# Attention and a two-layer network on one core: the first batch's q and k loaded in 2 KB runs and laid side by side by GpSimd

## The chip, the cores and the metric

The kernel runs on one core of one Trainium2 chip. The metric is the device time of one execution in microseconds, as the median of several runs. All arithmetic is 32-bit; matrix products run on TensorE (PE in the profile), the rest on VectorE (DVE), ScalarE (ACT) and GpSimd (POOL); SyncE (SP) issues nearly all loads and stores.

## What is computed

For 8 batches with 8 heads, 576 positions and 64 dimensions, two attentions are added: one over q, k and v averaged in groups of 4 (144 positions, its output repeated 4 times), and one over the 7 nearest positions. The result, 4608 rows of 512, goes through a layer of 2048 with a slope per column for negative values, and back to 512.

```python
q_d = q.reshape(B, H, Sd, 4, D).mean(axis=3)          # k_d, v_d alike
out_up = np.repeat(sm_attn(q_d, k_d, v_d), 4, axis=2)
mask = np.abs(pos[:, None] - pos[None, :]) < 4
scores = np.where(mask, scale * q @ k.T, -1e9)
out_local = softmax(scores) @ v
x = (out_up + out_local).transpose(0, 2, 1, 3).reshape(B * S, H * D)
h = x @ w_in
g = np.maximum(h, 0.0) + alpha * np.minimum(h, 0.0)
return g @ w_out
```

## The kernel before

**The steady part.** The 4608 rows go through the network in 18 chunks of 256 rows, each in 8 steps of 256 hidden columns: `hidden` (24 matmuls into h), `slopes` on ACT, `larger`, `split` into a high and a low part (gh, gl), `product` (24 matmuls into o). The weights are kept as high and low parts (wih, wil, woh, wol). They come as 64-bit numbers: `load_raw` brings a raw block (raw, 1 MB), and `make` turns it into the two parts: the absolute value on ACT (temp), two steps on DVE in `reach` (L198, L199), two in `bits` (L203, L204), the rounding on ACT (wih or woh, L209 or L213), the rest on DVE (wil or wol). Beside the matmuls run the attention of the later batches: `down` loads two heads' q, k and v (ld), adds them in fours on POOL (L74; s2q, s2k, s2v), and does the coarse attention; `local` does the near attention in units of 192 positions, mostly on DVE (qk, ls, lb, pv, x, xf).

**The first batch** is done ahead of all that by `first_batch`, as matrix products in four pairs of heads. For a pair hp, `load_pair` loads q and k of both heads into one tile fqk, so that the two heads' 64 dimensions lie side by side for each position, and v into fv; `load_windows` loads v once more in windows of 70 positions (vw). Then `pair`: fqk is transposed on PE (f0T for q, f1T for k); ACT copies it out into qb and kT; the near scores fs are 18 matmuls over a mask already in the bank; the coarse sums of q and k are adds on DVE (L466, L468), those of v L484 and L486; softmax (fmx, fp, fsm on DVE, exp on ACT), transposes (fpt, pT), the products with v (fdv, fpv), and the high and low parts xh and xl of the network's input.

**What sets the order.** The start, up to step 14, is not in a fixed order: a scheduler arranges each engine's queue by its own estimates, within what buffers and data allow. The loads are written in the order of `ORDER` ('i0 a0 a1 b0 o0 a2 b1 a3 b2 i1 b3 o1 i2': i and o are raw blocks of the input and output weight, a is `load_pair`, b is `load_windows`). Every engine works through its queue strictly in order, and SP holds a load until its buffer is free. From step 14 on the written order holds.

Of the kernel before, what the change touches and what calls it, by code (L numbers as in the profile page):

```python
# [9 lines left out]
F32 = mybir.dt.float32  # L10
# [13 lines left out]
HEAD = S * D  # L24
# [4 lines left out]
NWIN, WIN, KEYS = 9, 64, 70  # L29
# [23 lines left out]
def tile_attention_moe(ctx: ExitStack, tc: tile.TileContext, q, k, v, w_in, w_out, alpha, out):  # L53
    nc = tc.nc
# [3 lines left out]
    two = ctx.enter_context(tc.tile_pool(name="two", bufs=2))  # L58
# [80 lines left out]
    raws, turns = {}, [0, 0]  # L139
    weights_temp = []  # L140

    def load_raw(which, fp, blocks=(0, 1)):
        raw = raws.setdefault((which, fp), {})
        if fp < NP - 2:
            raw[None] = one.tile([128, 1024, 2], I32, tag=f"slot{turns[0] % 3}", name=f"raw{which}_{fp}")
            raw[0], raw[1] = raw[None][:, 0:512], raw[None][:, 512:1024]
            turns[0] += 1
        src = (w_in, w_out)[which].bitcast(I32)
        for c in blocks:
            if fp < NP - 2:  # L150
                dst = raw[None][:, 512 * c:512 * c + 512]
            elif fp == NP - 2:
                dst = raw[c] = late.tile([128, 512, 2], I32, tag="prod", name=f"raw{which}_{fp}{c}", bufs=PB)
            else:
                dst = raw[c] = late.tile([128, 512, 2], I32, tag=f"x{'hl'[c]}", name=f"raw{which}_{fp}{c}")
            if which == 0:
                nc.sync.dma_start(dst.rearrange("p (k a) b -> p k (a b)", k=2),
                                  bass.AP(src.tensor, 256 * c * 2 * DF + 512 * fp, [[2 * DF, 128], [256 * DF, 2], [1, 512]]))
            else:
                row = 256 * fp + 128 * c  # L160
                nc.sync.dma_start(dst.rearrange("p a b -> p (a b)"), src[row:row + 128, :])

    def weight_tiles(which, n):
        if n == 0 or (wi, wo)[which][0][n] is not None:
# [211 lines left out]
    def first_batch(st):  # L376
# [23 lines left out]
        qk, vt, vw = {}, {}, {}  # L400

        def load_pair(hp):
            qk[hp] = one.tile([72, 2, 8, 2, 64], F32, tag=f"spare{(4, 5, 0, 1)[hp]}", name=f"fqk{hp}")
            for i, src in enumerate((q, k)):
                for e in range(2):
                    nc.sync.dma_start(qk[hp][:, i, :, e, :],  # L406
                                      bass.AP(src.tensor, (2 * hp + e) * HEAD, [[512, 72], [64, 8], [1, 64]]))
            vt[hp] = st.tile([72, 2, 8, 64], F32, tag="vt", name=f"fv{hp}", bufs=3)
            nc.sync.dma_start(vt[hp].rearrange("p h t d -> p h (t d)"),
                              bass.AP(v.tensor, 2 * hp * HEAD, [[512, 72], [HEAD, 2], [1, 512]]))  # L410

        def load_windows(hp):
            vw[hp] = one.tile([KEYS, NWIN, 2, 64], F32, tag=f"spare{(6, 7, 2, 3)[hp]}", name=f"vw{hp}")
            for h2 in range(2):
                h = 2 * hp + h2
                if h == 0:
                    nc.vector.memset(vw[hp][0:3, 0, 0, :], 0.0)
                    nc.sync.dma_start(vw[hp][3:KEYS, 0, 0, :], bass.AP(v.tensor, 0, [[64, KEYS - 3], [1, 64]]))
                    nc.sync.dma_start(vw[hp][:, 1:, 0, :], bass.AP(v.tensor, (WIN - 3) * 64,
                                                                   [[64, KEYS], [WIN * 64, NWIN - 1], [1, 64]]))  # L420
                else:
                    nc.sync.dma_start(vw[hp][:, :, h2, :], bass.AP(v.tensor, h * HEAD - 3 * 64,
                                                                   [[64, KEYS], [WIN * 64, NWIN], [1, 64]]))

        def pair_bank(kind, name):
# [6 lines left out]
        def pair(hp):  # L432
# [100 lines left out]
            yield  # L533

        return load_pair, load_windows, pair


# [328 lines left out]
    with tc.tile_pool(name="start", bufs=1) as start:  # L866
        load_pair, load_windows, pair = first_batch(start)
        todo = [(w, fp) for fp in range(NP) for w in range(2)]
        for step in ORDER.split():
            kind, i = step[0], int(step[1])  # L870
            if kind in "io":
                load_raw("io".index(kind), i)
            else:
                (load_pair if kind == "a" else load_windows)(i)
        weights_temp.append(one.tile([128, 2, 1024], I32, tag="slot3", name="temp"))
        for hp in range(4):
            for _ in pair(hp):
                pass
        for fp in range(NP - 2):
            for which in range(2):  # L880
                if fp < N_EARLY:
                    if (which, fp) not in raws:
                        load_raw(which, fp)
                    for f in make(which, fp):
                        f()
        events = []

        def at(t, f, *args):
            events.append((t, len(events), f, args))

        down(1, 0, FIRST[0], 0.0, early=True)
# [12 lines left out]

    blocks = [(w, fp, c) for w in range(2) for fp in range(N_EARLY, NP) for c in range(2)]
    at(-1.98, load_raw, 0, N_EARLY)
    for fp in (NP - 2, NP - 1):
        at(-1.97, load_raw, 0, fp)
    at(-1.96, load_raw, 1, N_EARLY)
    t = T0_DEC  # L910
# [7 lines left out]
    for p in range(4 * (B - 1)):  # L918
        b, hp = 1 + p // 4, p % 4
# [17 lines left out]
    for u in range(3, 3 * B + 1):  # L937
# [7 lines left out]
        elif put:  # L945
            flip_at(u - 1, 0, begin[u] + 0.3, flip)
            put(0, when["before 0"])
            t = when["before 0"] + 0.25 if u == 4 else when["before 1"]
# [63 lines left out]
```

## Time and profile before

| | |
|---|---|
| median of 3 runs | 988.4 us (986.08 to 989.0) |
| profiled execution | 990.46 us, its span 988.6 us |
| PE busy | 948.9 us (96%) |
| DVE busy | 826.3 us (84%) |
| ACT busy | 557.7 us (56%) |
| POOL busy | 512.5 us (52%) |
| loads and stores | 98.28 MB in 63197 packets, 23556 of them under 512 bytes |
| mean granted TensorE clock | 0.972 |

Names in the profile are those of the tiles, without buffer numbers; a line number is that of the program printed above. Rows of stages give the stage, then busy time and number of instructions of PE, of PE's weight loads, of DVE, ACT and POOL, then the granted TensorE clock, the busy share of the DMA engines and GB/s. Rows of waits give who waited for whom: microseconds in total, how often, the longest. Rows of groups give busy time and mean nanoseconds; rows of one tile give the shortest, median and longest duration in nanoseconds; rows of the timeline give start and duration in microseconds and, in brackets, the idle time before and what ended it.

### The profile page before, as it was taken

To read this page: it belongs to the slowest core of one execution; us is meant where nothing else is said; L and a number is where in the kernel's file an instruction comes from. 1 tells how busy PE (TensorE), PEld (TensorE's weight loads), DVE (VectorE), ACT (ScalarE), POOL (GpSimd) and SP (SyncE) were. 2 spreads that over 40 slices of the span, in tenths; PEclk is the share of its full clock that TensorE was granted. 3 is DMA by queue.
4 is the path that set the end of the run, shared out by engine and by line. 5 is a ranking of instruction groups with operands and counts; after the bars stand their busy time and mean duration, and the time that the engine had idled before them with its cause. 6 is when DMAs were issued, how large, how long until landed. Compare 5 with 4: busy or idle time off the path is not lost.

```text
span 988.6 us, 17971 instructions
## 1 busy us (share of the span) xinstructions
PE 948.9 (96%) x6402; PEld 851.2 (86%) x6402; DVE 826.3 (84%) x1336; ACT 557.7 (56%) x1483; POOL 512.5 (52%) x624
## 2 busy tenths in 40 slices
PE   5986899799999999999999999999999999999998
PEld 4865798699889998989988989999899988999997
DVE  6799988979988898998989889899898889997111
ACT  4666876445656564655555555555646564444442
POOL 2184766657566545655546455555466633323221
PEclk9956899989999999999999999999999999999999
DMA  8944833223433323342313332322333311310000
GB/s 197 230 155 148 278 96 110 68 79 97 126 120 95 90 89 95 91 136 75 125 59 96 101 122 72 122 77 85 115 102 99 119 47 57 102 33 22 1 22 22
DMA packets 63197, 98.28 MB, mean 99 GB/s; under 512 B 23556, under 2 KB 28932, under 8 KB 63108
## 3 DMA queue, kind: packets, MB, share of 16 engines
q1 hardware_dynamic: 62916, 96.88, 32.9%
q8 instruction: 50, 0.82, 0.4%
q10 hardware_dynamic: 192, 0.26, 0.1%
q14 instruction: 39, 0.32, 0.1%
HBM read 87.67 MB, written 9.44 MB: 98 GB/s over the span
## 4 chain that ended last, share of the span: by engine, by line
PE 81%; DVE 8%; DMA 3%; POOL 2%; ACT 2%; SPq 2%; issue 2%; DVEq 0%; ACTq 0%; POOLq 0%
PE h L767 37%; PE o L824 37%; PE s L273 2%; PE pv L307 2%; DVE lb L663 1%; PE xp L672 1%; PE pT L297 1%; DVE qk L604 1%; DVE pv L660 1%; DMA ld<-in_q 1%; POOL ld L74 1%; SPq L406 1%; DMA ld<-in_v 1%; PE qkT L260 1%; DMA raw<-in_moe_w_out 1%
## 5 line engine op out<-in xcount | busy, mean ns | idle before, releaser
L71 POOL TENSOR_TENSOR gl<-t,gh 128x512 fp32r<-128x512 f32 x144 | 186.6, 1296 | 342.0 <-ACT gh L795 323.2
L778 ACT ACTIVATE t<-h,slope 128x256 f32<-128x256 f32 x288 | 136.6, 474 | 137.9 <-PE h L767 106.5
L767 PE MATMUL h<-xh,wih 128*128 128x256 f32 x1152 | 189.2, 286 | 10.1 <-ACT sh L780 5.7
L824 PE MATMUL o<-woh,gh 128*128 128x512 f32 x576 | 192.2, 404 | 0.0
L824 PE MATMUL o<-woh,gl 128*128 128x512 f32 x576 | 185.7, 393 | 0.0
L824 PE MATMUL o<-wol,gh 128*128 128x512 f32 x576 | 185.5, 393 | 0.0
L767 PE MATMUL h<-xl,wih 128*128 128x256 f32 x1152 | 182.1, 280 | 0.9 <-POOL xl L71 0.9
L767 PEld LDWEIGHTS h<-xh,wih 128*128 128x128 f32 x1152 | 164.6, 191 | 20.5 <-ACT sh L780 5.9
L767 PE MATMUL h<-xh,wil 128*128 128x256 f32 x1152 | 182.2, 280 | 0.0
L790 DVE TENSOR_TENSOR t<-h,t 128x512 f32<-128x512 f32 x132 | 90.6, 686 | 96.3 <-ACT h L782 94.6
L74 POOL TENSOR_TENSOR ld<-ld 72x256 f32<-72x256 f32 x168 | 137.6, 822 | 51.5 <-DMA ld<-in_q 46.4
L795 ACT CAST gh<-t 128x512 fp32r<-128x512 f32 x144 | 89.3, 620 | 131.5 <-DVE t L790 101.6
L767 PEld LDWEIGHTS h<-xl,wih 128*128 128x128 f32 x1152 | 155.9, 191 | 1.4 <-POOL xl L71 1.1
L767 PEld LDWEIGHTS h<-xh,wil 128*128 128x128 f32 x1152 | 156.7, 191 | 0.3
L608 DVE TENSOR_REDUCE ls<-qk 128x12 f32<-128x768 f32 (+1 forms) x126 | 136.2, 1083 | 2.9
L824 PEld LDWEIGHTS o<-woh,gl 128*128 128x128 f32 x576 | 108.1, 188 | 24.0
L824 PEld LDWEIGHTS o<-wol,gh 128*128 128x128 f32 x576 | 107.8, 188 | 22.7
L663 DVE TENSOR_TENSOR lb<-lb,pv 128x384 f32<-128x384 f32 x202 | 113.9, 564 | 5.6
L782 ACT ACTIVATE h<-h,sign 128x256 f32<-128x256 f32 x264 | 116.0, 439 | 0.0
L824 PEld LDWEIGHTS o<-woh,gh 128*128 128x128 f32 x576 | 99.0, 188 | 15.9 <-issue 3.0
L660 DVE TENSOR_TENSOR pv<-v,lb 128x1152 f32<-128x1152 f32 x84 | 93.6, 1114 | 2.6
L604 DVE TENSOR_TENSOR qk<-k,qp 128x768 f32<-128x768 f32 (+1 forms) x78 | 83.7, 1076 | 0.0
(151 smaller groups left out, 1154.9 us busy)
## 6 DMA issues: line engine op xcount, KB each, us to landing
k<-in_k SPq DMA_DIRECT2D x41, 384.0 KB
v<-in_v SPq DMA_DIRECT2D x41, 384.0 KB
out<-sg SPq DMA_DIRECT2D x140, 64.0 KB
raw<-in_moe_w_in SPq DMA_DIRECT2D x16, 512.0 KB
raw<-in_moe_w_out SPq DMA_DIRECT2D x16, 512.0 KB
ld<-in_q SPq DMA_DIRECT2D x56, 144.0 KB
ld<-in_k SPq DMA_DIRECT2D x56, 144.0 KB
ld<-in_v SPq DMA_DIRECT2D x56, 144.0 KB
```

Source lines behind the costliest of these rows:

```text
L71: nc.gpsimd.tensor_tensor(o, a, b, op=ALU.subtract)
L74: nc.gpsimd.tensor_tensor(o, a, b, op=ALU.add)
L604: nc.vector.tensor_tensor(st["pr"][:, :nd], window(tiles[u, "k"], half, d0, nd), st["qp", half].unsqueeze(1).to_broadcast([128, nd, 2, 192 ...
L608: nc.vector.tensor_reduce(out=st["s"][:, half, d0:d0 + nd, :].rearrange("p a b -> p (a b)"), in_=st["pr"][:, :nd].rearrange("p a h (t d) - ...
L660: nc.vector.tensor_tensor(st["pr"][:, :nd], window4(tiles[u, "v"], half, d0, nd), prob(half, d0, nd), op=ALU.mult)
L663: nc.vector.tensor_tensor(st["acc"], st["acc"], st["pr"][:, i], op=ALU.add)
L767: nc.tensor.matmul(ph[:, j], w[:, m, 128 * o:128 * o + 128], x[:, m, :], start=(i == 0), stop=(i == 11))
L778: nc.scalar.activation(t[:, j], hs[st][:, j], AF.Copy, scale=slope[:, f:f + 1])
L782: nc.scalar.activation(other[:, j], hs[st][:, j], AF.Copy, scale=sign[:, f:f + 1])
L790: nc.vector.tensor_tensor(gs[st], hs.pop(st), gs[st], op=ALU.max)
L795: nc.scalar.copy(gh, t)
L824: nc.tensor.matmul(outs[c][m], g[:, j, 128 * m:128 * m + 128], wo[w][n][:, o, :], start=(f == 0 and i == 0), stop=(f == NF - 1 and i == 2))
```

## The change

`load_pair` no longer brings q and k of a head into their place in fqk, 64 numbers at a time. Each of its 16 loads brings 72 rows of 512 numbers into a tile row as they lie in memory, and a copy on POOL puts them into fqk. The row tiles take turns in the buffers of gh, gl and t, which are not yet in use: two each, six in all. The loads of the first batch and the raw blocks of `ORDER`, and the copies, are pinned to the written order; the other loads of the start are not.

```diff
+    pinned = [True]
+
+    def load(dst, src):
+        ins = nc.sync.dma_start(dst, src)
+        if pinned[0]:
+            tc.keep_in_program_order(ins)
...
         def load_pair(hp):
             qk[hp] = one.tile([72, 2, 8, 2, 64], F32, tag=f"spare{(4, 5, 0, 1)[hp]}", name=f"fqk{hp}")
             for i, src in enumerate((q, k)):
                 for e in range(2):
-                    nc.sync.dma_start(qk[hp][:, i, :, e, :],
-                                      bass.AP(src.tensor, (2 * hp + e) * HEAD, [[512, 72], [64, 8], [1, 64]]))
+                    row = two.tile([72, 8, 64], F32, tag=("gh", "gl", "t")[(4 * hp + 2 * i + e) % 3], name=f"row{hp}{i}{e}")
+                    load(row.rearrange("p t d -> p (t d)"),
+                         bass.AP(src.tensor, (2 * hp + e) * HEAD, [[512, 72], [1, 512]]))
+                    tc.keep_in_program_order(nc.gpsimd.tensor_copy(qk[hp][:, i, :, e, :], row))
...
+        pinned[0] = False
         weights_temp.append(one.tile([128, 2, 1024], I32, tag="slot3", name="temp"))
```

The other loads of `load_raw`, `load_pair` and `load_windows` call load in place of nc.sync.dma_start. Lines behind the change move down by 7 to 10.

SP's queue at the very start, before (fqk0 is the first pair's q and k, fv0 its v, raw0_0 the first block of the input weight):

```order
L157 DMA raw0_0_151<-in_moe_w_in 128x2x512 x2
L406 DMA fqk0_154<-in_q 72x8x64 x2
L406 DMA fqk0_154<-in_k 72x8x64 x2
L409 DMA fv0_159<-in_v 72x2x512
L406 DMA fqk1_161<-in_q 72x8x64 x2
L406 DMA fqk1_161<-in_k 72x8x64 x2
L409 DMA fv1_166<-in_v 72x2x512
L418 DMA vw0_168<-in_v 67x64
```

The same place now (row100 is the second pair's first q, row110 its first k; ld1_0 are loads of the second batch):

```order
L145 DMA raw0_0_151<-in_moe_w_in 128x2x512 x2
L145 DMA row000_155<-in_q 72x512
L145 DMA row001_158<-in_q 72x512
L145 DMA row010_161<-in_k 72x512
L145 DMA row011_164<-in_k 72x512
L145 DMA fv0_167<-in_v 72x2x512
L145 DMA row100_170<-in_q 72x512
L145 DMA row101_173<-in_q 72x512
L249 DMA ld1_0_0_952<-in_q 72x512
L249 DMA ld1_0_1_957<-in_q 72x512
L249 DMA ld1_0_2_961<-in_k 72x512
L145 DMA row110_176<-in_k 72x512
```

Three loads of the second batch moved ahead of the second pair's k, which is the first load that has to wait for a row buffer.

POOL's queue behind the building of the masks, before:

```order
L109 MEMSET pat_r_962 128x6
L74 TENSOR_TENSOR ld1_0_0_920<-ld1_0_0_920 72x2x128
L74 TENSOR_TENSOR ld1_0_1_925<-ld1_0_1_925 72x2x128
L74 TENSOR_TENSOR s2q1_0_922<-ld1_0_0_920 72x2x64
L74 TENSOR_TENSOR ld1_0_2_929<-ld1_0_2_929 72x2x128
```

And now:

```order
L109 MEMSET pat_r_994 128x6
L416 COPY fqk0_154<-row000_155 72x8x64
L416 COPY fqk0_154<-row001_158 72x8x64
L416 COPY fqk0_154<-row010_161 72x8x64
L416 COPY fqk0_154<-row011_164 72x8x64
L416 COPY fqk1_169<-row100_170 72x8x64
L416 COPY fqk1_169<-row101_173 72x8x64
L74 TENSOR_TENSOR ld1_0_0_952<-ld1_0_0_952 72x2x128
L74 TENSOR_TENSOR ld1_0_1_957<-ld1_0_1_957 72x2x128
L74 TENSOR_TENSOR ld1_0_2_961<-ld1_0_2_961 72x2x128
L416 COPY fqk1_169<-row110_176 72x8x64
```

The copies stand where POOL went on to the second batch's adds, and three of those adds stand between the second pair's q and k.

ACT's queue in the first pair, before (f0T and f1T are the transposed q and k, wih0 the first block of the input weight):

```order
L442 COPY qb_143<-f0T00_209 64x9x8x4 x2
L442 COPY qb_143<-f0T04_216 64x9x8x4 x2
L446 COPY kT_146<-f1T00_223 128x72x4
L446 COPY kT_146<-f1T04_229 128x72x4
L209 CAST wih0_73<-temp_208 128x4x256
L442 COPY qb_143<-f0T10_361 64x9x8x4 x2
```

And now:

```order
L451 COPY qb_143<-f0T00_241 64x9x8x4 x2
L451 COPY qb_143<-f0T04_248 64x9x8x4 x2
L216 CAST wih0_73<-temp_240 128x4x256
L455 COPY kT_146<-f1T00_255 128x72x4
L455 COPY kT_146<-f1T04_261 128x72x4
L201 ACTIVATE temp_240<-raw1_0_189 128x1024
```

The weight's rounding moved ahead of the two copies of k, and the output weight's first block comes right behind them. DVE's queue moves likewise: the sums of the first v (L493, L495, formerly L484, L486) stand ahead of those of q.

More of the change, by code (lines that the diff above doesn't have):

```diff
@@ L156, in load_raw @@
             if which == 0:
-                nc.sync.dma_start(dst.rearrange("p (k a) b -> p k (a b)", k=2),
+                load(dst.rearrange("p (k a) b -> p k (a b)", k=2),
                                   bass.AP(src.tensor, 256 * c * 2 * DF + 512 * fp, [[2 * DF, 128], [256 * DF, 2], [1, 512]]))
@@ L160, in load_raw @@
                 row = 256 * fp + 128 * c
-                nc.sync.dma_start(dst.rearrange("p a b -> p (a b)"), src[row:row + 128, :])
+                load(dst.rearrange("p a b -> p (a b)"), src[row:row + 128, :])
     def weight_tiles(which, n):
@@ L405, in load_pair @@
                 for e in range(2):
-                    nc.sync.dma_start(qk[hp][:, i, :, e, :],
-                                      bass.AP(src.tensor, (2 * hp + e) * HEAD, [[512, 72], [64, 8], [1, 64]]))
+                    row = two.tile([72, 8, 64], F32, tag=("gh", "gl", "t")[(4 * hp + 2 * i + e) % 3], name=f"row{hp}{i}{e}")
+                    load(row.rearrange("p t d -> p (t d)"),
+                         bass.AP(src.tensor, (2 * hp + e) * HEAD, [[512, 72], [1, 512]]))
+                    tc.keep_in_program_order(nc.gpsimd.tensor_copy(qk[hp][:, i, :, e, :], row))
             vt[hp] = st.tile([72, 2, 8, 64], F32, tag="vt", name=f"fv{hp}", bufs=3)
-            nc.sync.dma_start(vt[hp].rearrange("p h t d -> p h (t d)"),
+            load(vt[hp].rearrange("p h t d -> p h (t d)"),
                               bass.AP(v.tensor, 2 * hp * HEAD, [[512, 72], [HEAD, 2], [1, 512]]))
@@ L417, in load_windows @@
                     nc.vector.memset(vw[hp][0:3, 0, 0, :], 0.0)
-                    nc.sync.dma_start(vw[hp][3:KEYS, 0, 0, :], bass.AP(v.tensor, 0, [[64, KEYS - 3], [1, 64]]))
-                    nc.sync.dma_start(vw[hp][:, 1:, 0, :], bass.AP(v.tensor, (WIN - 3) * 64,
+                    load(vw[hp][3:KEYS, 0, 0, :], bass.AP(v.tensor, 0, [[64, KEYS - 3], [1, 64]]))
+                    load(vw[hp][:, 1:, 0, :], bass.AP(v.tensor, (WIN - 3) * 64,
                                                                    [[64, KEYS], [WIN * 64, NWIN - 1], [1, 64]]))
                 else:
-                    nc.sync.dma_start(vw[hp][:, :, h2, :], bass.AP(v.tensor, h * HEAD - 3 * 64,
+                    load(vw[hp][:, :, h2, :], bass.AP(v.tensor, h * HEAD - 3 * 64,
                                                                    [[64, KEYS], [WIN * 64, NWIN], [1, 64]]))
```

## Prediction

> **What bounds the kernel now.** I read the slices of the page first, then the stages they suggest, then the waits. The slices: PE at nine tenths or more in most of the run, weak only in its first sixth; DMA full in the first two slices, the first 49 us.
>
> ```profile
> PE   5986899799999999999999999999999999999998
> DVE  6799988979988898998989889899898889997111
> DMA  8944833223433323342313332322333311310000
> ```
>
> The stages of the start and of the seam behind it, with DVE's busy time third:
>
> ```profile
> 8.94:52.00 43.06, 38.97 (x256) 34.50 (x256) 34.19 (x64) 26.56 (x72) 5.43 (x5) 1.00 0.92 214
> 50.00:70.00 20.00, 16.43 (x120) 13.05 (x116) 20.00 (x33) 14.59 (x37) 19.17 (x12) 0.57 0.45 146
> 52.00:98.00 46.00, 35.67 (x234) 29.05 (x228) 45.48 (x71) 29.66 (x75) 29.87 (x20) 0.55 0.47 152
> 96.00:197.50 101.50, 90.24 (x601) 80.54 (x599) 91.03 (x130) 67.22 (x171) 69.04 (x80) 0.96 0.45 142
> ```
>
> From 8.94 us, when DVE's first weight conversion starts, to 52 us DVE idles 43.06 - 34.19 = 8.9 us, and the DMA engines are 0.92 busy. From 52 to 98 us DVE is full (45.48 of 46.00): whatever it is spared before 52 us shortens the start one for one. What PE waits longest for once its steady stream has begun, in its timeline (the bracket is the idle time before and what ended it):
>
> ```profile
> 193.57 0.32 PE L260 MATMUL qkT<-ident,s2q 72*128 72x72 f32 x2 [2.07 <-DVE xf L684]
> 198.00 1.22 PE L767 MATMUL h<-xh,wih 128*128 128x256 f32 x4 [3.99 <-ACT xh L698]
> ```
>
> Both waits, from 191.5 to 198 us, end with DVE's first unit of the second batch (xf, which ACT rounds to xh). So up to about 197 us the time follows DVE's queue, not PE's: a DVE that is earlier shortens the run by up to 2.07 + 3.99 = 6.1 us, and a PE that alone is earlier only waits longer there. DVE's own waits from 8.9 to 98 us, ACT's one for the early output weight, and one of DVE's from 96 to 198 us (last row):
>
> ```profile
> DVE fv L484 <- DMA fv<-in_v: 4.2, 2, 2.2
> DVE rest L525 <- PE fpv L522: 1.7, 1, 1.7
> DVE fmx L494 <- PE fs L458: 0.8, 1, 0.8
> ACT temp L194 <- DMA raw<-in_moe_w_out: 0.9, 1, 0.9
> DVE x L666 <- POOL pv L74: 1.1, 1, 1.1
> ```
>
> Waits for loads are 4.2 + 0.9 = 5.1 us; the others come from the chain PE, ACT, DVE through the pairs of heads.
>
> **The loads.** Removed: 16 loads in runs of 256 bytes; added: 16 of the same bytes in runs of 2 KB. First row: the rate over the first 10 us in steps of 0.25 us, where the 2 KB runs of the first weight go first (values up to 418) and q and k follow (213 to 218 in the middle of the tail). Then SP's issue of the old loads, of loads with the new shape, and of the second input weight.
>
> ```profile
> GB/s 0 0 0 0 0 0 0 1 1 8 5 8 10 156 123 82 172 295 352 377 418 369 393 418 410 361 255 226 214 218 213 218 213 217 213 190 201 192 182 205
> L406 SPq DMA_DIRECT2D fqk<-in_q x8: 794/804/2403, 3.1 to 25.2; - x8
> L406 SPq DMA_DIRECT2D fqk<-in_k x8: 792/1070/3250, 5.0 to 28.8; - x8
> L242 SPq DMA_DIRECT2D ld<-in_q x6: 300/326/872, 37.4 to 96.7; - x6
> 31.44 0.99 SPq L157 DMA_DIRECT2D raw<-in_moe_w_in  x2
> ```
>
> 16 loads of 144 KB are 2.36 MB: 11.0 us at 215 GB/s, 6.0 us at 390, so 5.0 us of a full queue go. SP issues them in 16 x 0.33 = 5 us, not 8 x 0.80 + 8 x 1.07 = 15 us. Queued behind them on SP are the v tiles, the windows and the weights, so those land earlier, and I take the 5.1 us of waits for them as gone.
>
> [...]
>
> Three loads of the second batch (ld) now go ahead of the second pair's k, since those k rows wait for row buffers: 3 x 144 KB at 390 GB/s are 1.1 us. What hides it: the second pair's k is transposed only behind the first pair's scores. The pin itself costs nothing: SP had the written order before.
>
> **The copies on POOL.** Added: 16 copies of 72x512. No copy of this shape is in the trace. The nearest rows: a one-input operation, 64x630; an add of 72x256 in the steady state (734 ns) and in the start (median 1703); two of these adds that took longest beside a full DVE; and how long POOL has nothing to do.
>
> ```profile
> L382 POOL TENSOR_SCALAR_AFFINE_SELECT wpat<-wpat 64x630 f32<-64x630 f32 x2 | 1.5, 762 | 0.1
> L74 POOL TENSOR_TENSOR ld<-ld x113: 719/734/753, 300.8 to 794.5; 72x256 f32<-72x256 f32 x113
> L74 POOL TENSOR_TENSOR ld<-ld x15: 716/1703/3096, 46.6 to 102.4; 72x256 f32<-72x256 f32 x15
> 54.96 5.35 POOL L74 TENSOR_TENSOR ld<-ld 72x256 f32<-72x256 f32 x2
> POOL ld L74 <- DMA ld<-in_q: 40.0, 1, 40.0
> ```
>
> Lower end: 0.76 x 512/630 = 0.62 us. Upper end: 5.35/2 = 2.7 us. POOL is 1703/734 = 2.3 times slower beside a full DVE; in the first 50 us DVE is four fifths busy (34.19 of 43.06), so I take about twice the lower end, 1.2 us. 16 x 1.2 = 19 us lie in POOL's 40 us of idleness. Their cost is what waits for them:
>
> ```profile
> 9.36 1.19 PE L438 MATMUL f0T<-ident,fqk 72*128 72x72 f32 x8 [9.36 <-DMA fqk<-in_q]
> 9.67 0.69 DVE L199 TENSOR_SCALAR temp<-temp 128x1024 int32<-128x1024 int32 x1
> 10.96 1.22 DVE L203 SCALAR_TENSOR_TENSOR temp<-raw,temp 128x1024 int32<-128x1024 int32 x1
> 11.24 1.31 PE L438 MATMUL f1T<-ident,fqk 72*128 72x72 f32 x8
> 11.99 1.06 ACT L446 COPY kT<-f1T 128x288 f32<-128x288 f32 x2 [0.23 <-PE f1T L438]
> 12.43 0.68 DVE L484 TENSOR_TENSOR fv<-fv 72x512 f32<-72x512 f32 x1
> 13.64 1.22 DVE L204 SCALAR_TENSOR_TENSOR temp<-raw,temp 128x1024 int32<-128x1024 int32 x1
> 14.77 0.41 DVE L486 TENSOR_TENSOR fvd<-fv 72x256 f32<-72x256 f32 x1
> 14.89 1.04 ACT L209 CAST wih<-temp 128x1024 fp32r<-128x1024 f32 x1 [1.83 <-DVE temp L204]
> ```
>
> The first pair's q (0.29 MB) lands 0.29/215 - 0.29/390 = 0.6 us sooner, at 8.7. Four copies end at 8.7 + 4.8 = 13.5; k's transposes could begin there, and kT 0.8 later (11.24 to 11.99). But ACT now has the weight's rounding (wih) ahead of the two kT copies, and that waits for DVE, whose new order is L199 to 10.36, then fv 0.68, first bits 1.22, fvd 0.41, second bits 1.22: 13.9. wih ends at 14.9, so kT begins at 14.9, not at 11.99: the first pair is 2.9 us late, by ACT's order, and the copies stay just inside (8.7 + 4c + 0.8 for the transposes is below 14.9 up to c = 1.35). What is queued behind it, the score matmuls and all later pairs, shifts with it; I charge it in full, since DVE in the new order soon wants the first maximum.
>
> The row buffers are six, so the seventh row load waits for the first copy (9.9), and the 13th for the seventh copy, which stands behind three adds: 8.7 + 7 x 1.2 + 3 x 1.7 = 22.2. SP holds everything behind it, but the second input weight would still be issued at about 28, not 31.44: no cost.
>
> POOL beside DVE also slows DVE: in 50 to 70 us POOL is busy 19.17, and two of DVE's operations there stand well over their usual time (usual, then slowed):
>
> ```profile
> 26.16 0.80 DVE L501 TENSOR_TENSOR fp<-fp,frs 128x630 f32<-128x630 f32 x1
> L501 DVE TENSOR_TENSOR fp<-fp,frs 128x630 f32<-128x630 f32 x1 | 1.3, 1334 | 0.0
> L468 DVE TENSOR_TENSOR fs2k<-fqk 72x256 f32<-72x256 f32 x4 | 1.9, 478 | 0.0
> L468 DVE TENSOR_TENSOR fs2q<-fqk 72x256 f32<-72x256 f32 x1 | 0.9, 943 | 0.0
> ```
>
> That is 0.53 + 0.47 = 1.0 us for 19 us of POOL, and the copies are 19 us: +1.0.
>
> **The sum.** -5.1 + 2.9 + 1.0 = -1.2 us on DVE's queue, all inside the 6.1 us that PE waits for it. The profiled execution has a span of 988.6 and 990.46 in all, 2.06 above the median 988.4 of the three runs: 989.3 for it, 987.2 for the median. No change can be told here below 0.3%, 3.0 us.
>
> **Rivals.** *Faster: the delay of the first pair is absorbed.* DVE's queue then holds work that needs no k (the second input v, the early output weight). If that fills the 2.9 us, the waits go at no price; and since the seam's SP order now has the second batch's loads ahead of the stores, the 1.1 us for POOL's pv goes too: -5.1 - 1.1, so the 6.1 that PE can give: 982.3. For it: 5.1 of the 8.9 us of idleness are loads. Against it: the others are this very chain.
>
> *Slower: the copies are slow.* At c = 2.7 kT begins at 8.7 + 10.8 + 0.8 = 20.3, 8.3 us late: 8.3 + 1.0 - 5.1 = +4.2, 992.6. It turns the sign from c = 1.65 and passes 3 us at c = 2.4. For it: the adds' median of 1703 ns has half the elements of a copy. Against it: a copy has one input, and DVE is less full at 9 us than at 50. [...]
>
> *Nothing moves.* The waits for loads turn into waits for PE and ACT of the same length: 988.4.
>
> **Numbers.** Forecast 0.36; nothing moves 0.06; faster rival 0.34; slower rival 0.24. Faster 0.34, same 0.42, slower 0.24. The range reaches a little past both rivals, 981 to 993; the forecast's own is 985.4 to 990.
>
> **What would show it.** Right: no wait of DVE for fv; kT's first copy near 15 us; copies near 1.2 us; DVE's idleness from 9 to 52 us near 7.5 us; PE's wait for xh or xf near 195 us shorter by a microsecond. Wrong: copies over 2 us with SP held behind them, or DVE idleness under 5 us.

## The result: 6 us slower, and the profile after

| | before | after |
|---|---|---|
| median (lowest to highest of 5 runs each) | 988.4 us (986.08 to 989.8) | 994.39 us (992.53 to 995.05) |
| ratio, with its 95% interval | | 1.0066 [1.0043, 1.0089] |
| profiled execution, its span | 990.46 us, 988.6 us | 994.39 us, 992.1 us |

The two profiled executions differ by 3.9 us, the medians by 6.0: before's profiled execution was one of its slower ones.

The slices of after, PE in tenths, as in the prediction for before:

```profile
PE   3887799989999999999999999999999999999998
```

PE is weaker in its first two slices (3 and 8, were 5 and 9), and from the tenth on all is full in both: the loss is in the start. Its first stage in after, with busy time and count of PE, PE's weight loads, DVE, ACT, POOL, then clock, DMA share and GB/s:

```profile
9.00:52.00 43.00, 31.73 (x181) 27.55 (x181) 34.12 (x53) 21.76 (x58) 23.20 (x24) 1.00 0.89 217
```

Up to 52 us PE has issued 181 matmuls (256 before) and DVE 53 operations (64 before). DVE idles 43.00 - 34.12 = 8.9 us, as much as before: the waits that should vanish were replaced, and its operations are fewer and longer. The DMA engines move 217 GB/s; before it was 214. What waits for what from 8.5 to 52 us in after, a choice of rows (total, times, longest):

```profile
ACT temp L201 <- DMA raw<-in_moe_w_out: 6.4, 1, 6.4
DVE temp L205 <- ACT temp L201: 5.0, 2, 2.9
DVE fv L493 <- DMA fv<-in_v: 2.1, 3, 1.0
```

DVE's wait for fv went from 4.2 to 2.1. But ACT's wait for the output weight went from 0.9 to 6.4, and DVE, behind ACT, waits 5.0 us for the weight's absolute value (2.4 before). The same place in the timelines of after: SP, ACT, DVE, PE.

```profile
14.62 3.08 SPq L145 DMA_DIRECT2D raw<-in_moe_w_out  x2
...
16.77 0.79 ACT L455 COPY kT<-f1T 128x288 f32<-128x288 f32 x2
23.98 1.12 ACT L201 ACTIVATE temp<-raw 128x1024 f32<-128x1024 f32 x1 [6.42 <-DMA raw<-in_moe_w_out]
...
15.59 1.09 DVE L475 TENSOR_TENSOR fqk<-fqk 72x512 f32<-72x512 f32 x1
16.71 0.83 DVE L477 TENSOR_TENSOR fs2q<-fqk 72x256 f32<-72x256 f32 x1
25.13 0.73 DVE L205 TENSOR_SCALAR temp<-temp 128x1024 f32<-128x1024 f32 x1 [2.87 <-ACT temp L201]
25.78 0.65 DVE L503 TENSOR_REDUCE fmx<-fs 128x7 f32<-128x490 f32 x1
28.49 0.78 DVE L493 TENSOR_TENSOR fv<-fv 72x512 f32<-72x512 f32 x1 [0.41 <-DMA fv<-in_v]
...
17.69 0.47 PE L482 MATMUL fsum<-ident,fs2q 72*128 72x72 f32 x2 [4.07 <-ACT kT L455]
17.95 4.05 PE L467 MATMUL fs<-kT,qb 128*128 128x70 f32 x18
33.33 4.11 PE L467 MATMUL fs<-kT,qb 128*128 128x70 f32 x18 [1.19 <-ACT kT L455]
```

The output weight is issued at 14.62 (before at 14.50) and lands at 23.98 (before at 22.79). The times of landing are read here from the start of ACT's step that waits for it. In the new order ACT takes this weight ahead of the rest of the first pair (qd, at 25.00 instead of 18.62, and fkd) and of the second pair's qb, and DVE's first maximum of the first pair stands behind the weight's first step. The same rows of before:

```profile
14.50 2.12 SPq L161 DMA_DIRECT2D raw<-in_moe_w_out  x2
...
18.62 0.58 ACT L476 ACTIVATE qd<-fsum 64x144 f32<-64x144 f32 x2
22.79 1.12 ACT L194 ACTIVATE temp<-raw 128x1024 f32<-128x1024 f32 x1 [0.89 <-DMA raw<-in_moe_w_out]
...
13.11 4.11 PE L458 MATMUL fs<-kT,qb 128*128 128x70 f32 x18
25.85 4.11 PE L458 MATMUL fs<-kT,qb 128*128 128x70 f32 x18 [0.90 <-ACT kT L446]
```

So before used the time until 22.79 for the first pair. The first pair's scores are 4.8 us late in after (13.11 to 17.95), the second pair's 7.5 (25.85 to 33.33), the third pair's 8.2 (40.95 to 49.15).

How that reaches the end: from PE's first product with an output weight (o) on, nearly all kernels here need nearly the same time. It starts at 108.56 of 988.6 us in before and at 113.93 of 992.1 in after: 880.0 and 878.2 us remain. In the kernels profiled below that remainder lies between 877.5 and 881.1, except in e16, whose start the scheduler arranged anew (871.0). So, but for e16, the span is set by when PE leaves the start. That place in before's chain of waits (pieces between left out), with POOL's and PE's row of it; then in after's timelines:

```profile
85.14 4.53 DMA ld<-in_k
94.11 0.88 POOL s2k L74
95.00 0.30 SPq L242
95.41 3.64 DMA raw<-in_moe_w_in
...
84.59 1.37 POOL L74 TENSOR_TENSOR s2q<-ld 72x128 f32<-72x128 f32 x2 [12.87 <-PE qkT L260]
102.30 1.22 PE L767 MATMUL h<-xh,wih 128*128 128x256 f32 x4 [5.70 <-ACT sh L780]
```

```profile
85.97 4.55 POOL L74 TENSOR_TENSOR s2q<-ld 72x128 f32<-72x128 f32 x2 [22.10 <-PE qkT L267]
97.09 1.43 POOL L74 TENSOR_TENSOR s2k<-ld 72x128 f32<-72x128 f32 x1
98.55 0.30 SPq L249 DMA_DIRECT2D ld<-in_q  x1
102.98 0.62 ACT L201 ACTIVATE temp<-raw 128x512 f32<-128x512 f32 x1 [5.15 <-DMA raw<-in_moe_w_in]
104.07 1.23 PE L314 MATMUL pv<-th,s2v 72*64 72x144 f32 x8 [6.25 <-ACT th L308]
106.39 1.23 PE L776 MATMUL h<-xh,wih 128*128 128x256 f32 x4 [0.42 <-ACT sh L789]
113.93 0.50 PE L833 MATMUL o<-woh,gh 128*128 128x512 f32 x1 [1.58 <-ACT gh L804]
```

A load of the second batch (ld) waits for POOL's adds to free its buffer; SP holds a block of the input weight behind it; ACT waits for that block, with the slopes and the copy th behind it, and PE for these: 5.70 us at h in before, 6.25 at pv in after. The steady h begins at 102.30 before and at 106.39 after.

This chain starts later in after. SP issues the block at 98.95 instead of 95.41. Of these 3.5 us, 1.4 lie ahead of POOL's adds s2q (85.97, was 84.59), and 2.0 in the first of the two, which takes 2.5 us where before has 0.5. That is no accident of one execution: in every profiled kernel with the old order at this place (before, e1, e3, e5, e6, e7, e9, e11, e12) the two adds take 1.37 to 1.39 us, in every listed or pinned one with the new order there 3.16 to 4.62. The adds are the same; the order of DVE's operations beside them is not. That this makes the difference is argued from these rows, not tested by itself. In after the first o waits 1.58 us more for gh, which stands behind POOL's adds of the next ld.

### The profile page after: what moved, and what is told of

The parts are those of the page before. It is cut to its first block, busy times and chain, and to the rows that moved or that the text cites. A ratio compares the mean times of both kernels' runs of the same rounds, so it can differ in the third digit from the quotient of the medians.

```text
span 992.1 us, 18003 instructions
## 1 busy us (share of the span) xinstructions
PE 943.6 (95%) x6402; PEld 845.8 (85%) x6402; DVE 827.0 (83%) x1336; ACT 557.5 (56%) x1483; POOL 524.1 (53%) x640
## 4 chain that ended last, share of the span: by engine, by line
PE 80%; DVE 9%; DMA 4%; POOL 3%; issue 2%; ACT 1%; SPq 0%; DVEq 0%; POOLq 0%; ACTq 0%
PE o L833 36%; PE h L776 35%; PE s L280 2%; DMA ld<-in_q 2%; PE pv L314 1%; DVE lb L672 1%; PE xp L681 1%; DVE qk L613 1%; PE pT L304 1%; PE fs L467 1%; DVE ls L617 1%; DVE pv L669 1%; POOL ld L74 1%; DMA vw<-in_v 1%; DMA raw<-in_moe_w_out 1%
## 5 line engine op out<-in xcount | busy, mean ns | idle before, releaser
L74 POOL TENSOR_TENSOR ld<-ld 72x256 f32<-72x256 f32 x168 | 127.9, 764 | 28.3 <-DMA ld<-in_k 16.9
```

What stands on the lines that cost most here:

```text
L74: nc.gpsimd.tensor_tensor(o, a, b, op=ALU.add)
```

## The experiments

To change loads and order apart from each other, the experiments write out the order of the start for each engine as a list: an edge from each instruction to the next, which is meant to set the order of issue and add no wait. e6, before under its own list, took 988.9 us in one execution, where before's beside it had a median of 987.32.

```diff
+    for engine, text in TABLE.items():        # TABLE: one list of instruction numbers for each engine
+        mine = [x for x in nc.cur_bb.bb.instructions if str(x.engine).endswith(engine) ...]
...
+        for a, z in zip(row, row[1:]):
+            tc.add_manual_dep(mine[z], mine[a].name, mybir.DependencyInfo(
+                mybir.DependencyClass.NoSync, mybir.DependencyReason.DATA), reason="listed")
```

"Old order" is before's order of the five engines so listed, "new order" after's.

### Loads or order: e1, e2, and before listed (e6)

e1 has the new loads and copies in the old order, e2 the old loads in the new order, e6 is before held by the list.

> The loads in 2 KB runs and GpSimd's 16 copies of the changed kernel, but every engine of the arranged start kept in the order of the kernel before (the copies ahead of GpSimd's first add). Theory A, the order: the copies and the loads cost nothing, the changed order of ScalarE and VectorE costs the 6 us (ACT holds the second pair's work behind the wait for the first output weight, which lands at 24 us as before): 984 to 989, and the second pair's scores start at 24 to 27 us instead of 33.3. Theory B, the copies: they slow DVE and hold the loads behind the row buffers, whatever the order: 992 to 996. Theory C, the loads are worth something and the order eats it: below 986.

> The loads of the kernel before (pieces of 256 bytes, no copies), but every engine of the arranged start in the order of the changed kernel. Theory A, the order: as slow as the changed kernel or slower, 992 to 1000, with ACT's wait of 6 us or more for the first output weight. Theory B, the copies: like the kernel before, 986 to 990.

> The kernel before with its own order written out as a list: the same instructions in the same order. A second look at its profile, to see how much its places in the start move from run to run. All theories: 985 to 990; the end of DVE's 134 operations at 94 to 98 us (97.80 in the first look, which was 2 us above the median).

e1 took 988.12 us, ratio 1.0004 [0.9987, 1.0020]; e2 991.32, 1.0043 [1.0023, 1.0062]; e6, seen once, 988.9. (The runs were made in groups on several chips. The ratio is taken to the executions of before beside each run, whose medians were 986.0 to 988.4 us; it is not the quotient of two medians of this text.) The new order loses with the old loads too, and the new loads lose nothing in the old order: the order is the cause. Whether the loads and copies add to the loss in the new order cannot be told, since the intervals of e2 and after overlap. e1 met the 984 to 989 that were expected if the order is the cause; e2 stayed just below its 992 to 1000, but ACT again waits for the output weight, as expected, at the same place:

```profile
ACT temp L194 <- DMA raw<-in_moe_w_out: 6.4, 1, 6.4
```

DVE does the same 134 operations from its first weight step to the last one ahead of its first half-width weight block. The stretch they take, in rows like those above (DVE's busy time is third), for before, e6, after, e1 and e2:

```profile
8.94:97.80 88.86, 74.64 (x484) 63.55 (x484) 79.67 (x134) 56.22 (x146) 35.10 (x24) 0.77 0.69 181
```
```profile
9.00:96.42 87.42, 69.62 (x484) 57.98 (x484) 80.92 (x134) 56.35 (x146) 27.48 (x24) 0.75 0.72 184
```
```profile
9.14:101.33 92.19, 68.41 (x484) 58.05 (x484) 82.31 (x134) 56.35 (x148) 44.75 (x39) 0.91 0.63 172
```
```profile
9.30:93.99 84.69, 67.97 (x484) 57.23 (x484) 83.17 (x134) 55.95 (x146) 52.77 (x39) 0.76 0.69 188
```
```profile
8.71:100.92 92.21, 68.43 (x484) 58.08 (x484) 80.39 (x134) 56.40 (x148) 26.58 (x24) 0.90 0.64 175
```

Length less DVE's busy time is what DVE idles: 9.2 and 6.5 us in the two profiled executions of before's order (before and e6), 9.9 in after, 1.5 in e1, 11.8 in e2. So with the old order the loads do what the prediction asked of DVE's waits and more, without a gain in the median, and with the new order the idleness is back. DVE's busy time for these operations is 79.67 and 80.92 us in before and e6 and 80.39 in e2, and with the copies 82.31 in after and 83.17 in e1: 1.4 to 3.5 us more. The 2.7 us of idleness between before and e6 are the spread of one and the same order, and a warning: part of the 5.1 us of waits that the prediction took away may have been particular to one execution. e1's profiled execution (985.56) was likewise one of its fastest, so that its early end of the stretch promises more than its median of 988.12 keeps.

### Without the copies: e3, e5

e3 loads in 2 KB runs but lays nothing side by side: the heads are transposed one by one. e5 loads the runs into fqk as they lie.

```diff
-                    nc.sync.dma_start(qk[hp][:, i, :, e, :],
-                                      bass.AP(src.tensor, (2 * hp + e) * HEAD, [[512, 72], [64, 8], [1, 64]]))
+                    nc.sync.dma_start(qk[hp][:, i, 4 * e:4 * e + 4].rearrange("p t h d -> p (t h d)"),   # e5
+                                      bass.AP(src.tensor, (2 * hp + e) * HEAD, [[512, 72], [1, 512]]))
```

> Loads in 2 KB runs straight into the tile, the two heads one behind the other, so no copies at all; PE turns each head by itself (128 matmuls of 64 columns instead of 64 of 128), DVE adds the same elements in other places; the order of the kernel before on every engine. Theories A and B both expect the loads' gain without a price: 983 to 987, about the 4 us of DVE's waits for loads. Theory D, the loads bind nothing, because what is queued behind them waits for other things: 987 to 990.

> Loads in 2 KB runs straight into the q and k tiles, no copies: the laying of two heads side by side is left out, every other instruction keeps its shape, and all engines keep the order of the kernel before. It shows the loads' gain without GpSimd's price. Theory A, the copies give the gain back by slowing DVE (in the run with copies in the old order DVE's first 134 operations took 4.0 us more than in the kernel before, and waited 7.7 less): DVE idle 1.5 to 3 us up to its first 512-column weight operation instead of 9.2, slowed as in the kernel before (4.5), the end of these 134 at 90 to 92 us, time 981 to 985. Theory D, the loads bind nothing: 987 to 990, with the idleness as before.

e3 took 991.99 us, 1.0047 [1.0025, 1.0070], and missed its expectation: the 128 half-width transposes fill PE in the start.

```profile
9.00:52.00 43.00, 41.53 (x450) 35.26 (x449) 34.74 (x65) 27.87 (x74) 2.31 (x3) 1.00 0.93 209
```

450 matmuls stand there for 256, busy 41.5 of 43 us: another bound, no evidence on the copies. e5 took 986.53 us, 0.9987 [0.9969, 1.0006], between its two theories, although DVE's stretch ended at 92.85, 5 us sooner than in before. Part of that goes into one wait of PE:

```profile
98.64 1.22 PE L767 MATMUL h<-xh,wih 128*128 128x256 f32 x4 [8.08 <-ACT sh L780]
```

It is the chain through ld, SP and the input weight shown above. PE's wait there is 8.1 us, where before has 5.7 and e6 6.6, and o begins at 104.83, 3.7 us sooner than in before. So 3.7 of the 5 us reach o in the profiled execution, and of the 0.8 us between the medians (987.32 for before beside it) nothing can be told.

### Which place of the order: e4, e13, e10, e11, e14, e17, e18

e4 puts ACT's rounding of the first input weight behind the kT copies, and the first output weight's operations on ACT and DVE, with the third v's sum, behind the first pair's fp. e13 puts that rounding and DVE's operations up to the first input weight's lower half into their old places, so that the sums of q stand ahead of the weight's bits. e10 keeps the old order on every engine up to the second pair's scores; both go on in the new order, and e11 is the reverse of e10. e14 makes the first output weight from the first input weight's block, so nobody waits for it; e17 takes e14 and moves the third v's sum behind the first softmax and the second pair's sum of q; e18 adds e13's moves to e17.

```diff
  # ACT's queue, e4 against after
  qb x4
- wih
  kT x2
- temp (output weight)
+ wih
  qd x2, fkd, qb x4, fp
+ temp (output weight)
```

```diff
  # e14: raw block of the first output weight
-            st["raw"] = raws[which, fp].pop(c).rearrange("p (k a) b -> p k a b", k=k)
+            tile_ = raws[which, fp].pop(c)
+            if (which, fp) == (0, 0):
+                raws["first"] = tile_
+            elif (which, fp) == (1, 0):
+                tile_ = raws["first"]
+            st["raw"] = tile_.rearrange("p (k a) b -> p k a b", k=k)
```

> The changed kernel in its own order but for one thing: the first output weight's operations of ACT and DVE (and the wait for its load, and the third input v's) put behind the first pair's softmax and the second pair's q, and the first input weight's rounding behind the two kT copies. Theory A, the order of this weight: back to 986 to 990, second pair's scores at 24 to 28 us. Theory B, the copies: 992 to 996. If the rest of the order matters as much: 990 to 993.

> The changed kernel in its own order, but DVE's first operations up to the first input weight's lower half as in the kernel before (the first pair's q sums ahead of the weight's bits) and ACT's rounding of that weight behind the two kT copies. The first pair's scores begin at about 15 us instead of 17.95 in both theories. Theory F1, the first pair's lateness is what is lost: 989 to 991.5. Theory F2, the wait for the first output weight (lands at 24 us), which stands ahead of the second pair's work on ACT and of the first maximum on DVE, holds the second pair all the same (scores at 32 to 33.5 us): 993 to 995.

> The changed kernel (its loads and copies); up to the second pair's scores and the first output weight (about the first 32 us) every engine in the order of the kernel before, from there in the changed kernel's order. Theory F, the order of the first 32 us loses the time: 986 to 989, like the old order throughout. Theory G, what loses it is the later order (the phase of the weights on DVE against GpSimd's adds and the exit): 991 to 995.

> The reverse: the changed kernel with its own order up to the second pair's scores and the first output weight, from there the order of the kernel before. Theory F: 991 to 995, like the changed kernel. Theory G: 986 to 989.

> The changed kernel in its own order, but the first output weight is made from the first input weight's tile, which is there already (its own load is still issued and never read): the wait for a landing at 24 us is taken away and nothing is moved. Theory F, this wait ahead of the second pair's work on ACT and of the first maximum on DVE is what the new order loses: the second pair's scores at 27 to 30 us instead of 33.3, time 988 to 991. If other places of the order lose it: 993 to 995.

> As the run that takes away the wait for the first output weight, and besides the third input v's sum on DVE (whose load lands at 28 to 30 us) put behind the first pair's softmax and the second pair's q sums; everything else in the changed kernel's order. Theory F, the new order loses by putting the consumers of late loads ahead of the pairs: second pair's scores at 28 to 30 us instead of 33.3, time 988 to 991. Theory G, the time does not hang on the second pair at all: scores earlier, time 992 to 995.

> The same, and DVE's first operations up to the first input weight and ACT's rounding behind the kT copies as in the kernel before, so that the first pair begins at 15 us: the head of the new order with all three of its known waits gone. Theory F: second pair's scores at 26 to 28 us, 986 to 990. Theory G: 991 to 995.

| new loads, and | median us | ratio to before | scores of pair 1 and 2 at |
|---|---|---|---|
| new order (after) | 994.39 | 1.0066 [1.0043, 1.0089] | 17.95, 33.33 |
| weights behind the pair (e4) | 993.92 | 1.0063 [1.0040, 1.0086] | 17.83, 34.72 |
| old in ACT and DVE for pair 1 (e13) | 992.23 | 1.0042 [1.0025, 1.0058] | 15.18, 33.59 |
| old to pair 2 (e10) | 990.33 | 1.0027 [1.0007, 1.0046] | 15.46, 26.34 |
| new to pair 2, then old (e11) | 993.45 | 1.0072 [1.0047, 1.0097] | 18.12, 33.33 |
| all old (e1) | 988.12 | 1.0004 [0.9987, 1.0020] | 14.87, 25.74 |
| no wait for the weight (e14) | 993.52 | 1.0070 [1.0050, 1.0090] | second 35.60 |
| nor for the third v (e17) | 990.33 | 1.0008 [0.9985, 1.0031] | second 29.40 |
| e17 with an earlier first pair (e18) | 990.95 | 1.0030 [1.0008, 1.0052] | 14.27, 26.89 |

e4 refutes what the prediction named: with wih out of the way kT is ready at 14.04, and the first pair's scores still begin at 17.83, because the PE instruction ahead of them is the sum fsum, which waits for DVE's sum of q (L475 and L477, 15.59 to 17.54 in after), and these stand behind the weight's bits in DVE's new order. ACT's next rows wait for fsum too, until 22.72, behind DVE's sum of k (to 22.12; e4's rows of waits):

```profile
ACT qd L485 <- PE fsum L482: 6.1, 1, 6.1
```

e14 likewise: without ACT's wait for the output weight, DVE runs on and meets the third pair's v, which it reads ahead of the second half of the first pair's fp:

```profile
30.86 0.69 DVE L498 TENSOR_TENSOR fv<-fv 72x512 f32<-72x512 f32 x1 [4.54 <-DMA fv<-in_v]
```

The medians fall as the old order reaches further (after, e13, e10, e1), but neighbouring intervals overlap, so the parts are not sized; e1 is told apart from after and from e13, no run from its neighbour. e11 shows that the old order behind the second pair mends nothing that can be seen once the two pairs are late. e18's earlier pairs, 2.5 us sooner in the second than e17's, brought nothing. Single places of the order were expected to bring it back, and did not: e4 missed its 986 to 990 and e14 its 988 to 991; e17 met its 988 to 991, e11 the 991 to 995 of an early loss; e10, e13 and e18 fell between their theories.

### The pin: e16, and after once more (e15)

e16 is after without the pin on the loads; the copies stay in the written order. e15 is after itself, beside it.

```diff
-    pinned = [True]
+    pinned = [False]
```

> The changed kernel without the pin on its loads: the row loads and the copies stay, and the scheduler also orders SP's queue. The first output weight's operations still stand ahead of the second pair's. Theory F: 991 to 996, as with the pin. Theory P, the pin is what costs: 986 to 989.

> The changed kernel once more, beside the others on one chip. All theories: 992 to 995.

e15 took 993.81 us, 1.0067 [1.0045, 1.0090]; e16 988.43, 1.0024 [1.0003, 1.0044]. The scheduler, free to order SP's queue, puts the output weight ahead of the second pair's k and the three loads of the second batch behind; the weight is issued from 11.82 and lands at 21.31, not 23.98. The intervals of e15 and e16 just part, so most of the loss hangs on the pin on the loads.

By what way is another matter. In e16 the pairs are late as well (scores at 18.71 and 35.39), and o begins at 112.56, hardly sooner than in after. What is gone are PE's waits for xf and xh near 195 us, 2.3 and 2.6 us in after; the longest wait of PE from 110 us on is now this:

```profile
PE h L776 <- POOL xl L71: 0.8, 1, 0.8
```

So neither earlier pairs nor the exit of the start give e16 its gain (its profiled execution, 985.64, is one of its faster ones), but an order in which DVE has done more by then: 165 operations up to 112.56 us, 158 in after. What the earlier output weight has to do with that is open. That the pin makes the scheduler order ACT and DVE otherwise is seen; which rule of the scheduler does it is not shown, and no run pins before's loads or frees the copies.

### How the start is left: e7, e9, e12, e19

One block of the input weight (two loads) is issued ahead of the ld load that waits for POOL. e7 does so in before (old order), e9 in e1, e12 in e5 (no copies), e19 in after.

```diff
  # SP's queue
  ld<-in_v x2
+ raw<-in_moe_w_in x2
  ld<-in_q
- raw<-in_moe_w_in x2
  ld<-in_q
```

> The kernel before in its listed order, with one change on SP: the two loads of the sixth input weight ahead of the third down-sampled pair's first q load, which waits for GpSimd. Theory E, the exit of the start is this chain (GpSimd's adds, SP, the weight's landing at 99.1, PE's wait of 5.7 us): the weight lands 4 us sooner, PE starts again at 98 to 99 instead of 102.3, time 984 to 986. If VectorE's queue binds by itself: 987 to 989.

> The changed kernel's loads and copies in the order of the kernel before, with the same change on SP. Theory E: 984 to 986, as the same change on the kernel before, if loads and copies cancel; 981 to 984 if VectorE's earlier end (94.0 against 97.8 in the first looks) is real. If VectorE's queue binds by itself: 985 to 988.

> The loads in 2 KB runs without copies (heads not laid side by side), in the old order, with the sixth input weight's loads ahead on SP. With the copies this gave 982.9. If GpSimd's copies cost time through DVE (4 us more of DVE's time in the traces) once the exit is free: 979 to 981. If that cost lies beside other waits: 982 to 984.

> The changed kernel in its own order, with the sixth input weight's loads ahead of the third down-sampled pair's first q load on SP. In the order of the kernel before this gave 1.1 us without and 4 to 5 us with the new loads. Theory E, the start leaves through this chain in every order: the weight lands 4 us sooner and the first matmul of the second product starts 3 to 4 us sooner, 989 to 991. If the changed kernel's start leaves through another chain: 993 to 995.

e7 took 986.24 us, 0.9976 [0.9958, 0.9994]; e9 982.92 (982.25 to 986.12), 0.9958 [0.9941, 0.9975]; e12 981.50, 0.9962 [0.9935, 0.9988]; e19 986.82, 0.9999 [0.9979, 1.0019]. e9 met its 981 to 984, e19 came out better than its 989 to 991, e7 and e12 fell between their theories. So the move alone takes after back to before: ACT's wait for the block fell from 5.15 to 0.30 us (first row, e19), and o begins at 108.32 instead of 113.93. But it does not take the order's loss away: e19 and e9 have the same loads, copies and move and differ in the order, and their intervals do not overlap. In e9, which keeps the copies, PE waits 1.9 us where before waits 5.7, and o starts at 99.69 instead of 108.56 (last rows).

```profile
98.28 0.63 ACT L201 ACTIVATE temp<-raw 128x512 f32<-128x512 f32 x1 [0.30 <-DMA raw<-in_moe_w_in]
```
```profile
94.45 0.74 PE L776 MATMUL h<-xh,wih 128*128 128x256 f32 x4 [1.94 <-ACT sh L789]
99.69 0.50 PE L833 MATMUL o<-woh,gh 128*128 128x512 f32 x1 [1.18 <-ACT gh L804]
```

e9 beats both kernels. e12 differs from e9 by the copies alone, and their medians, 1.4 us apart, are not told apart by their intervals: the copies cost no time that these runs can see, though 2 us would be hidden in them.

## Why the prediction was wrong, step by step

- **Loads behind land earlier, -5.1 us: failed in the order that was built.** The output weight was issued at 14.62 instead of 14.50 and landed 1.2 us later, and the third v, issued 2.8 us sooner (19.74, was 22.52), still made DVE wait (28.49). No freed queue shows: from 9 to 52 us the engines moved 217 GB/s against 214. The three ld loads, which the prediction costed at 1.1 us and hid behind the second pair's k, held up everything behind them: the output weight goes at 14.62, and at 13.48 in e1, where they come later. In the old order (e1) the same loads leave DVE 1.5 us of idleness up to 94 us: the waits went, and the median stayed at 988.12. So the 5.1 us were there to be had on DVE's queue, but in the order that was built they were replaced by waits for other things, and where they were had they were not time.
- **"The pin itself costs nothing": failed.** It compared SP's rows before and after and not what the scheduler does with the other engines once SP's queue is fixed. e16 against e15 shows the cost, 0.4% of the time by their ratios.
- **First pair late by 2.9 us: right in sign, mis-sized and wrongly put.** kT began at 16.77 for 14.9 (11.99 before), since DVE's first two steps took 1.12 and 0.98 us beside the copies (0.69 each before) and it then waited 0.68 us for fv. The order rows showed ACT's wih ahead of kT and the sums of v ahead of those of q. The prediction used both for when wih is ready, but not that the sums of q now end at 17.54 and that fsum on PE, ahead of the scores, waits for them. It also read the place where the output weight stands behind kT, and did not ask when that load lands: 6.4 us of ACT, with the second pair behind it.
- **Copies 1.2 us each: right.** Their row in after (shortest, median, longest):

```profile
L416 POOL COPY fqk<-row x16: 605/1021/2203, 8.4 to 34.6; 72x512 f32<-72x512 f32 x16
```

  The ends of 0.62 and 2.7 us were fair for single copies. The slower rival, copies at 2.7 us, came nearest to the time (992.6 for 994.39) by a mechanism that did not occur; that is luck.
- **DVE slowed by 1.0 us: too small.** 1.4 to 3.5 us up to some 100 us, by whether before or e6 and which kernel with copies is taken; 2.6 between the two profiles that the prediction is about.
- **All of it inside the 6.1 us that PE waits near 195: failed.** Those waits in after (PE from 110 us on):

```profile
PE h L776 <- ACT xh L707: 2.6, 1, 2.6
PE qkT L267 <- DVE xf L693: 2.3, 1, 2.3
```

  They are 4.9 us for 6.1, shorter by the microsecond that was named as a sign of being right, and yet the time was longer: here it means that 1.2 us of a late start came back. Nor does an earlier DVE shorten these waits by itself: in e1, where DVE idles 7.7 us less than in before, they are 4.0 and 2.3 us. In all these kernels but e16 the time follows the chain that leaves the start (ld, SP, input weight, ACT, PE). Its wait of PE in before, 5.70 us at 102.30, is longer than either wait near 195, and the prediction did not read it. In after that chain came later: by 4.1 us at h, by 5.4 at o. Only in e16 do the waits near 195 go.

What stays open: how the loss divides among the places of the order, since single repairs (e4, e14) only moved the wait; which part of it is made at the exit, by POOL's adds; by what way the pin costs; and why executions of one program differ by several microseconds, with DVE idling 9.2 us in before and 6.5 in e6.

## What to carry to other kernels

A change to loads in front of a scheduler is two changes: cost the order it will build, and for every load that an engine reads ahead of other work ask when that load lands. Look for an instruction from which the rest of the run takes the same time in most versions (here the first o) and follow the chain that releases it; an engine freed earlier is worth little if that chain does not move. Test it on a version with another order, as e16 here, before it is called a rule. Where two executions of one kernel differ by more than the term you are adding up, that term needs a second look.

## What the runs showed of the hardware that was not expected

**DVE's steps took longer beside POOL's copies, and POOL's adds beside DVE's new order.** Mean durations from 8.5 to 52 us (in ns, the number ahead of the last bar), before and then after, of a step of DVE with one input and of one with two:

```profile
L199 DVE TENSOR_SCALAR temp<-temp 128x1024 int32<-128x1024 int32 x3 | 2.0, 667 | 0.0
L203 DVE SCALAR_TENSOR_TENSOR temp<-raw,temp 128x1024 int32<-128x1024 int32 x3 | 3.6, 1205 | 0.0
```
```profile
L206 DVE TENSOR_SCALAR temp<-temp 128x1024 int32<-128x1024 int32 x3 | 2.6, 866 | 0.0
L210 DVE SCALAR_TENSOR_TENSOR temp<-raw,temp 128x1024 int32<-128x1024 int32 x3 | 3.6, 1213 | 0.0
```

The first rose by 0.20 us beside POOL's copies, the 1.2 us step hardly at all; the number of inputs does not sort these rows, for DVE's adds of 72x512, with two, rose from 683 to 884 ns. At the exit POOL is the one that gets longer: its two small adds took 4.55 us (s2q at 85.97 in after) where before has 1.37, and DVE's steps beside them kept their usual 1.21 and 0.68 us. So it was not always the same engine that lost; what decides which one does, no run here shows.

**PE's waits at the exit could cost twice: the matmuls behind them ran at a granted clock of about half.** Granted clock (third number from the end) over the first h matmuls behind PE's wait at the exit: before (wait 5.7 us), e7 (3.3) and e9 (1.9):

```profile
102.30:107.71 5.41, 5.41 (x26) 5.26 (x28) 5.41 (x7) 4.10 (x9) 4.12 (x4) 0.52 1.05 391
```
```profile
99.11:101.84 2.73, 2.73 (x12) 2.73 (x13) 2.73 (x6) 2.40 (x5) 1.27 (x1) 0.50 0.85 257
```
```profile
94.45:97.47 3.02, 3.02 (x26) 2.89 (x28) 3.02 (x6) 2.40 (x5) 1.89 (x3) 1.00 0.59 170
```

The same 24 matmuls take 5.4 us behind before's wait, at a clock of 0.52, and 3.0 us behind e9's, at 1.00. In e19 no single wait of PE there is longer than 1.45 us, but from 97.94 to 101.73 us PE is busy for only 1.1, and the clock is 0.50 too:

```profile
101.73:107.22 5.49, 5.49 (x25) 5.49 (x26) 5.49 (x7) 2.37 (x6) 4.32 (x8) 0.50 0.77 257
```

Of the 8.9 us by which o starts sooner in e9 than in before, 3.8 are wait and 2.4 lie in these 24 matmuls. Behind 1.9 us of waiting the clock was 1.00, behind 3.3 us it was 0.50, and so it was behind the two short waits of e19 (1.45 and 1.24 us). In e12, behind a wait of 2.53 us, the groups of four of these matmuls that began at 93.97, 94.82 and 95.68 took 1.06, 1.05 and 1.06 us, where those last ahead of the wait took 0.62. The low clock lasted 2.7 us in e7 (from 101.84 to 103.50 it was 0.86), and over 5 us in before and e19. How long a wait it takes, and what brings the clock back, these rows do not show.
